# Scanning half as many time steps: odd times by recurrence, even times from them

## The chip, the cores and the metric

The kernel runs on one core of a Trainium2 chip. The metric is the device time of one execution in microseconds. A core has five engines with instruction queues of their own: TensorE (PE in the profile; PEld is its loading of weights), VectorE (DVE), ScalarE (ACT), GpSimd (POOL) and SyncE (SP), and 16 DMA engines that the queues feed. Matmuls write PSUM; the other engines copy results from there to SBUF.

## The reference

Two sequence models over the same input x (2048 times, 1024 channels) are mixed by a gate per time.

```python
def _A_ref(x, Lambda_re, Lambda_im, B_re, B_im, C_re, C_im, log_dt, Dskip):
    Lam, Bmat, Cmat = ...                      # complex
    Lam_bar = jnp.exp(jnp.exp(log_dt) * Lam)
    B_bar = ((Lam_bar - 1.0) / Lam)[:, None] * Bmat
    Bu = jnp.einsum("bld,pd->blp", x + 0j, B_bar)
    for t in range(L):
        h = Lam_bar[None, :] * h + Bu[:, t, :]
        hs.append(h)
    return 2.0 * jnp.einsum("blp,dp->bld", hseq, Cmat).real + x * Dskip[None, None, :]

def _B_ref(q, k, v, shift_k, ssm_k, ssm_D):
    kv = causal_conv4(k, shift_k) * v
    y = long_causal_conv(kv, ssm_k)            # the reference does it by FFT
    return q * (y + kv * ssm_D[None, None, :])

g = _sigmoid((x * gate_w).sum(-1, keepdims=True))
return g * a + (1 - g) * b                     # a = _A_ref(x, ...), b = _B_ref(x, B_k, B_v, ...)
```

The recurrence of `_A_ref` has 1024 complex states. The change concerns how these states are computed.

## The kernel before, in words

The kernel has two halves that overlap for some 40 us. `put` chains every instruction to the one before it on its engine, so each engine works in the order of the program.

**The convolution half** (to about 200 us) computes `_B_ref` by transforms that are matmuls, for eight blocks of 128 channels. `products` multiplies spectra on DVE, `inverse` transforms back (`psz` to `cv`), and the result goes to a scratch in DRAM (`cv_scr`). In the same loop `turn_table` (line 393) builds, for each of the eight groups of 128 states (`pi`), the tables `TC`, `TS` (cosine and sine of the turned angle at each of the 512 times of a block) and `TCi`, `TSi`, the same tables times the factor of the inputs (`c2r`, `c2i`). The latter need two products `m` and an accumulating DMA (`gather`) from POOL.

**The scan half** works on four time blocks `tb` of 512 times and four groups `g` of 256 states, so there are 16 scans.

- `Bu(tb, g)` (652): 32 matmuls of 512 columns on TensorE, 16 for each half `j` into one PSUM tile, and two copies by ACT into `U`. PSUM has four tiles of this size (`ps2`).
- `scan(tb, g, fin)` (663): DVE turns `U` by `TCi`, `TSi` (`A`), which makes the recurrence real; then four `tensor_tensor_scan` instructions of 512 columns (`W`); then it turns back by `TC`, `TS` into the states `hb`. `carry` brings the last state of a block into the next. `scan` is a generator: its steps interleave two scans on DVE. No instruction of ACT is in it.
- `Cy(tb, tl)` (755): 32 matmuls with the states of all four groups as weights, for 128 times, and a copy by ACT times the gate (`scale_a`).
- `scale_b` (ACT) and `finish` (DVE, POOL's DMA, output) mix in the other half; `gate` makes the gate; `load_xT` and `load_CT` are transposing DMAs on SP.

The order is written out by hand at the end: Bu(0,3), Bu(1,0), two gates, Bu(1,1) to Bu(1,3), then a loop over k of 12 passes, with scan k+4, Cy(k), `scale_b(k+1)` and Bu two blocks ahead. Bu ends in pass 7. The last time block's Cy is spread over its groups.

```python
    def advance(j):
        step(scans[j])
        if j + 1 < NS:
            step(scans[j + 1])
        run(scans[j])
    ...
        advance(k + NG)
        Cy(tb, st)
        if k + 1 < NS - NG:
            scale_b(k + 1)
        if tb + 2 < NTB:
            Bu(tb + 2, st)
```

Small tiles come from pools with a few buffers: `wu` (4, for `U` and others), `wk` (3, for the scan's intermediates), `hb` (8).

Of the kernel before, what the change touches and what calls it, by code (L numbers as in the profile page):

```python
# [20 lines left out]
def kernel(  # L21
# [43 lines left out]
    PAD = 16  # L65

# [10 lines left out]
    wu = pool("wu", 4)  # L77
# [60 lines left out]
    m_pool = h3pool(h3, "m", 1)  # L138
# [73 lines left out]
    def load_xT(tb, home=None, halves=(0, 1)):  # L212
        if 0 in halves:
            xTs[tb] = (home or xt_pool).tile([128, ND, TB], BF16, name="xT", tag="xT")
        for h in halves:
            t0 = tb * TB + h * 256
            load_t(xTs[tb][:, :, h * 256:(h + 1) * 256], xf[t0:t0 + 256, :])
# [119 lines left out]
    rv, thn, c2r, c2i, mc2i = small("rv"), small("thn"), small("c2r"), small("c2i"), small("mc2i")  # L337
    TCS = rot_pool.tile([128, NP, 2, TB], BF16, name="TCS")
    TCSi = rot_pool.tile([128, NP, 2, TB], BF16, name="TCSi")
    TC, TS = TCS[:, :, 0], TCS[:, :, 1]  # L340
    TCi, TSi = TCSi[:, :, 0], TCSi[:, :, 1]
# [7 lines left out]
    def state_params():  # L349

        dtv = small("dtv")
        act(dtv, logdt, func=ACT.Exp)
        abv = pair("abv")
        tt(abv, bc(dtv[:, None], [128, 2, NP]), pcol[:, 1:3], ALU.mult)
        act(rv, abv[:, 0], func=ACT.Exp)
        ts(thn, abv[:, 1], 1.0 / TWO_PI, None, ALU.mult)
# [23 lines left out]
        tt(e[:, 0], rv, co[:, 0], ALU.mult)  # L380
        tt(e[:, 1], rv, si[:, 0], ALU.mult)
        ts(e[:, 2], e[:, 0], -1.0, None, ALU.add)
        ts(e[:, 0], e[:, 0], -1.0, None, ALU.add)
# [6 lines left out]
        for o, i, f in ((c2i, p2, 2.0), (mc2i, p2, -2.0), (c2r, p1_, 2.0)):  # L390
            put("dve", V.scalar_tensor_tensor, out=o, in0=i[:, 0], scalar=f, in1=invden, op0=ALU.mult, op1=ALU.mult)

    def turn_table(pi, home):


        hr = home([128, 2, TB], F32, "hr")
        h, rq = hr[:, 0], hr[:, 1]
        act(h, trow[0], func=ACT.Identity, scale=thn[:, pi:pi + 1])
        act(rq, trow[0], func=ACT.Identity, scale=thn[:, pi:pi + 1], bias=magic)
# [5 lines left out]
        act(TS[:, pi], rq, func=ACT.Sin, scale=-TWO_PI)  # L405
        act(TC[:, pi], h, func=ACT.Sin, bias=pih, scale=-TWO_PI)
        yield
# [3 lines left out]
        yield  # L411
        act(flat(TCSi[:, pi]), flat(TCS[:, pi]), func=ACT.Identity, scale=c2r[:, pi:pi + 1])
        gather(flat(TCSi[:, pi]), flat(m))
# [4 lines left out]
    eos, kss = {}, {}  # L418

# [205 lines left out]
    hbs = {}  # L625
    WL, init = {}, {}
# [14 lines left out]
    def carry(tb):  # L641
        q1 = consts.tile([128, 2, NP], F32, name="q1", tag="q1")
        q2 = consts.tile([128, 2, NP], F32, name="q2", tag="q2")
        w = WL[tb - 1]
        tt(q1, w, bc(cs["cU"][:, None, :], [128, 2, NP]), ALU.mult)
        tt(q2, w, bc(cs["sU"][:, None, :], [128, 2, NP]), ALU.mult)
        tt(init[tb][:, 0], q1[:, 0], q2[:, 1], ALU.add)
        tt(init[tb][:, 1], q1[:, 1], q2[:, 0], ALU.subtract)

    Us = {}  # L650
# [12 lines left out]
    def scan(tb, g, fin):  # L663


        last = tb == NTB - 1 and g == NG - 1
        U = Us.pop((tb, g))
        A = w4([128, 2, 2, TB], BF16, "A")
        W = None

        for js in ([slice(0, 1), slice(1, 2)] if last else [slice(0, 2)]):
            g2 = slice(2 * g + js.start, 2 * g + js.stop)
            full = [128, 2, js.stop - js.start, TB]
            Aj, Uj = A[:, :, js], U[:, :, js]
            tt(Aj, bc(TCi[:, g2][:, None], full), Uj, ALU.mult)
            if js.start == 0:
                yield
            b = w4([128, 2, 2, TB], BF16, "trn")[:, :, js]
            tt(b, bc(TSi[:, g2][:, None], full), Uj, ALU.mult)
            if js.start == 0:  # L680
                if g == 0 and tb > 0:
                    carry(tb)
                step(fin)
            tt(Aj[:, 0], Aj[:, 0], b[:, 1], ALU.add)
            tt(Aj[:, 1], b[:, 0], Aj[:, 1], ALU.subtract)
            if W is None:
                W = w4([128, 2, 2, TB], BF16, "W")
            for j in range(js.start, js.stop):
                pi = 2 * g + j
                for c in range(2):  # L690
                    put("dve", V.tensor_tensor_scan, out=W[:, c, j], data0=bc(rv[:, pi:pi + 1], [128, TB]),
                        data1=A[:, c, j], initial=0.0 if tb == 0 else init[tb][:, c, pi:pi + 1],
                        op0=ALU.mult, op1=ALU.add)
            if js.start == 0:
                run(fin)
                hbs[tb, g] = s5p["hb"][(tb * NG + g) % 8 > 2].tile([128, 2, 2, TB], BF16, name="hb")
            hb = hbs[tb, g][:, :, js]
            Wj = W[:, :, js]
            tt(hb, bc(TC[:, g2][:, None], full), Wj, ALU.mult)
            if tb < NTB - 1:  # L700
                copy(WL[tb][:, :, g2], Wj[:, :, :, TB - 1])
            b = w4([128, 2, 2, TB], BF16, "trn")[:, :, js]
            tt(b, bc(TS[:, g2][:, None], full), Wj, ALU.mult)
            if not last:
                yield
            tt(hb[:, 0], hb[:, 0], b[:, 1], ALU.add)
            tt(hb[:, 1], hb[:, 1], b[:, 0], ALU.subtract)
# [6 lines left out]

    def loads(t_):
        rows = slice(t_ * 128, (t_ + 1) * 128)
# [20 lines left out]
    def Cy_g(tb, tl, ps, g, last, by_half=False):  # L737
        tsl = slice(tl * 128, (tl + 1) * 128)
# [22 lines left out]
    def finish(t_, ps=None):  # L761

        rows = slice(t_ * 128, (t_ + 1) * 128)
# [39 lines left out]
    copy(trow[0], iota_i32([128, TB], [[1, TB]], 0, 0, "row"))  # L803
# [115 lines left out]
    with tc.tile_pool(name="fin", bufs=1, side="right") as fin:  # L919
# [30 lines left out]
    def load_CT(pi):  # L950
        for c, src in enumerate((A_C_re, A_C_im)):
            load_t(CT[pi][:, c], src[:, pi * 128:(pi + 1) * 128])

    s5p = {}
    wk = pool("wk", 3)

    s5p["hb"] = pool("hb3", 3), pool("hb5", 5)
# [7 lines left out]
    for pi in range(NP):  # L965
        load_CT(pi)
    move(drow, bc(A_Dskip.rearrange("(o d) -> o d", o=1), [128, D]))
    loads(0)
    Bu(0, 3)
    Bu(1, 0)  # L970
    gate(0)
    gate(1)
    for g in range(1, NG):
        Bu(1, g)
    scale_b(0)

    NS = NTB * NG
    scans = [scan(j // NG, j % NG, finish(j - NG - 1) if j > NG else none) for j in range(NS)]

    def advance(j):  # L980
        step(scans[j])
        if j + 1 < NS:
            step(scans[j + 1])
        run(scans[j])

    step(scans[0])
    for j in range(NG):
        advance(j)
# [21 lines left out]
    pss = []  # L1010
    for tl in range(4):
        ps = ps2([128, 2, 512], "psy")
        halves = [(slice(h * 512, h * 512 + 512), ps[:, h]) for h in range(2)]
        pss.append(([ps[:, 0], ps[:, 1]], halves if tl == 3 else [(slice(0, D), flat(ps))]))
    for g in range(NG - 1):
        for tl in range(4):
            Cy_g(tb, tl, pss[tl][0], g, False)
    run(finish(t0 - 1))
    fins = []
    for tl in range(4):  # L1020
        fins.append(finish(t0 + tl, None if tl == 1 else pss[tl][1]))
        step(fins[tl])
    for tl in range(4):
        Cy_g(tb, tl, pss[tl][0], NG - 1, True, tl == 3)
        if tl == 1:
# [30 lines left out]
```

## Time and profile before

| | before |
|---|---|
| runs shown, median | 414.21 us |
| runs shown, lowest and highest | 414.06, 427.37 us |
| profiled execution, span from first to last instruction | 413.4 us |
| TensorE busy | 404.2 us, 2377 matmuls |
| VectorE busy | 398.3 us, 470 instructions |
| ScalarE busy | 254.9 us, 307 instructions |
| GpSimd busy | 52.4 us |
| mean granted TensorE clock | 0.999 |

The page gives the profiled execution's span and no other time of it; the median of the runs is 0.8 us above that span. Busy time counts the union of an engine's instructions. A profile line of a group reads: engine, operation, output and input by the program's names, shapes, count, then busy us, mean ns of one, and the idle time of the engine just before them with what ended it. A line of the timeline has its start and length first. `psy` are the matmuls of Cy, `bu` those of Bu, `psz` those of `inverse`. As one helper records all instructions of an engine, the line number says little and the tile names are read.

### The profile page before, as it was taken

What the parts mean: (1) busy time and instruction counts of PE and PEld (TensorE: products, weight loads), DVE (VectorE), ACT (ScalarE), POOL (GpSimd) and SP (SyncE); (2) the same over time, 40 slices, a digit from 0 to 9 for tenths busy, and PEclk for the clock granted to TensorE, in tenths of its full rate; (3) what the DMA queues carried; (4) which work ended last, traced back from release to release, by engine and by line L of the source; (5) the groups of instructions that cost most, each with busy time, mean ns of one, the idle gap of its engine ahead of it and who ended that gap; (6) DMA issues with size and microseconds to landing.
All of it is one profiled execution on the core that took longest, in us unless ns stands there. A gap on an engine that the chain in (4) does not pass through costs nothing.

```text
span 413.4 us, 6089 instructions
## 1 busy us (share of the span) xinstructions
PE 404.2 (98%) x2377; PEld 202.2 (49%) x2377; DVE 398.3 (96%) x470; ACT 254.9 (62%) x307; POOL 52.4 (13%) x74
## 2 busy tenths in 40 slices
PE   7999999999999999999999999999999999999995
PEld 4556454554646464444445444444444444444442
DVE  7899999999999999999999999999999999999964
ACT  4898979999999999889223235432542344387001
POOL 3010020202020202001000000101100110133100
PEclk9999999999999999999999999999999999999999
DMA  7768099998999994795199981533955564498422
GB/s 154 154 142 204 10 177 227 215 136 168 217 194 235 190 144 101 155 192 133 33 190 188 175 187 27 124 77 81 203 122 133 117 139 127 78 203 175 106 51 102
DMA packets 126302, 59.79 MB, mean 145 GB/s; under 512 B 106041, under 2 KB 112705, under 8 KB 126274
## 3 DMA queue, kind: packets, MB, share of 16 engines
q1 hardware_dynamic: 117664, 42.22, 47.2%
q0 software_dynamic: 8528, 17.17, 25.1%
q8 instruction: 18, 0.29, 0.3%
q14 instruction: 10, 0.08, 0.1%
q10 hardware_dynamic: 82, 0.02, 0.0%
HBM read 12.86 MB, written 8.39 MB: 51 GB/s over the span
## 4 chain that ended last, share of the span: by engine, by line
PE 64%; DVE 27%; issue 4%; ACT 2%; DMA 1%; ACTq 0%; DVEq 0%
PE psy L91 27%; PE bu L91 27%; DVE wkh L91 8%; DVE BT L91 7%; DVE G L91 6%; PE psz L91 5%; DVE t L91 3%; PE psk L91 2%; DVE ks L91 2%; PE taps L91 1%; DVE ev L91 1%; PE psv L91 1%; PE p L91 1%; DMA rows<-in_A_Lambda_im_dram 1%; PE foldk L91 1%
## 5 line engine op out<-in xcount | busy, mean ns | idle before, releaser
L91 PE MATMUL bu<-xT,BT 128*128 128x512 bf16 x512 | 112.5, 379 | 0.0
L91 PE MATMUL psy<-CT,hb 128*128 128x512 bf16 x512 | 112.0, 379 | 0.0
L91 PEld LDWEIGHTS <-BT 128*128 128x128 bf16 x512 | 50.0, 98 | 60.2
L91 PEld LDWEIGHTS <-hb 128*128 128x128 bf16 x512 | 49.9, 98 | 60.0
L91 ACT ACTIVATE U<-bu 128x1024 bf16<-128x1024 f32 x32 | 32.4, 1020 | 48.2 <-PE bu L91 45.8
L91 DVE TENSOR_TENSOR_SCAN W<-rv,init,A 128x512 bf16<-128x512 f32 x48 | 57.7, 1262 | 0.0
L91 PE MATMUL psz<-G,SI 128*128 128x512 bf16 x128 | 48.5, 379 | 1.9 <-DVE G L91 1.9
L91 PE MATMUL psz<-G,CI 128*128 128x512 bf16 x128 | 48.5, 379 | 0.0
L91 ACT ACTIVATE ga<-psy,gcols 128x1024 bf16<-128x1024 f32 x8 | 8.9, 1113 | 46.3 <-PE psy L91 46.3
L91 PE MATMUL taps<-dg,kT 128*128 128x128 bf16 x512 | 31.8, 226 | 0.0
L91 PEld LDWEIGHTS <-kT 128*128 128x128 bf16 x512 | 30.6, 101 | 0.7
L91 ACT ACTIVATE Vh<-psv 128x1024 bf16<-128x1024 f32 x32 | 30.3, 1041 | 0.0
L91 POOL DMA_DIRECT2D pbb<-gd x12 | 10.3, 856 | 131.5 <-ACT gd L91 119.4
L91 PE MATMUL psk<-eok,CF 128*128 128x512 bf16 (+1 forms) x96 | 25.7, 361 | 0.4 <-ACT eok L91 0.4
L91 PE MATMUL psk<-eok,SF 128*128 128x512 bf16 (+1 forms) x96 | 24.2, 361 | 0.0
L91 ACT ACTIVATE BT<-psy,gcols 128x1024 bf16<-128x1024 f32 x5 | 5.6, 1113 | 29.9 <-PE psy L91 29.9
L91 PEld LDWEIGHTS <-SF 128*128 128x128 bf16 x160 | 15.7, 98 | 16.0 <-issue 0.6
L91 PEld LDWEIGHTS <-CF 128*128 128x128 bf16 x160 | 15.3, 98 | 14.4
L91 DVE TENSOR_TENSOR wkh<-BT,Vh 128x3072 bf16<-128x3072 bf16 (+4 forms) x20 | 21.8, 1112 | 0.0
L91 DVE TENSOR_TENSOR wkh<-Kh,Vh 128x3072 bf16<-128x3072 bf16 (+2 forms) x16 | 21.3, 1352 | 0.0
L91 PEld LDWEIGHTS <-CI 128*128 128x128 bf16 x128 | 12.5, 98 | 17.9 <-issue 3.3
L91 DVE TENSOR_TENSOR hb<-TCS,W 128x2048 bf16<-128x2048 bf16 (+1 forms) x17 | 19.8, 1162 | 1.2
(148 smaller groups left out, 654.9 us busy)
## 6 DMA issues: line engine op xcount, KB each, us to landing
G<-wkh POOLq DMA_DIRECT2D x6, 768.0 KB, 7.2
cv_scr<-cv SPq DMA_DIRECT2D x16, 256.0 KB, 6.3
v<-in_B_v_dram SPq DMA_DIRECT2D x3, 1024.0 KB
pbb<-cv_scr SPq DMA_DIRECT2D x12, 256.0 KB, 3.2
xr<-in_A_x_dram SPq DMA_DIRECT2D x12, 256.0 KB, 3.6
pbb<-gd POOLq DMA_DIRECT2D x12, 256.0 KB, 3.9
TCSi<-m POOLq DMA_DIRECT2D x8, 256.0 KB, 7.5
ga<-xr POOLq DMA_DIRECT2D x8, 256.0 KB, 3.3
```

The costliest lines, as they stand in the source:

```text
L91: i = f(*a, **kw)
```

## The change

The recurrence now runs over the odd times of a block only (256 instead of 512), with the squared factor (`r2`): the input of an odd step is the odd U plus lambda times the even U before it. The even states come afterwards: the even U plus lambda times the odd state before. Both products with lambda (`by_lam`: R from U, ahead of the scan; Q from the odd states, behind it) are four ACT instructions of 512 columns each. The even states of scan i are finished (`evens`) on DVE inside scan i+1. The factor of the inputs, formerly in `TCi`, `TSi`, is multiplied into C once (`turn_C`: four `tensor_scalar` of 1024 columns on DVE and an accumulating DMA of 512 KB per state group). The times of a block are stored with even and odd times apart, so x is loaded, and the output stored, with every second row. C is loaded before the last `inverse`.

The diff, cut to its core:

```diff
-    wu = pool("wu", 4)
+    wu = pool("wu", 6)
 ...
-            load_t(xTs[tb][:, :, h * 256:(h + 1) * 256], xf[t0:t0 + 256, :])
+            load_t(xTs[tb][:, :, h * TH:(h + 1) * TH], xf[tb * TB + h:(tb + 1) * TB:2, :])
 ...
     def turn_table(pi, home):
-        m = m_pool.tile([128, 2, TB], BF16, name="m")
-        act(m[:, 0], TS[:, pi], func=ACT.Identity, scale=c2i[:, pi:pi + 1])
-        act(m[:, 1], TC[:, pi], func=ACT.Identity, scale=mc2i[:, pi:pi + 1])
-        act(flat(TCSi[:, pi]), flat(TCS[:, pi]), func=ACT.Identity, scale=c2r[:, pi:pi + 1])
-        gather(flat(TCSi[:, pi]), flat(m))
 ...
+    def turn_C(pi):
+        n = w4([128, 2, D], BF16, "n")
+        k = slice(pi, pi + 1)
+        for c in range(2):
+            ts(n[:, c], CT[pi][:, 1 - c], mc2i[:, k], None, ALU.mult)
+        for c, f in enumerate((c2r, mc2r)):
+            ts(CT[pi][:, c], CT[pi][:, c], f[:, k], None, ALU.mult)
+        gather(CT[pi].rearrange("p c d -> p (c d)"), n.rearrange("p c d -> p (c d)"))
 ...
+    def by_lam(o, src, g):
+        for q in range(2):
+            for j in range(2):
+                act(o[:, q, :, j], src[:, :, j], func=ACT.Identity, scale=cs["lam"][:, q, 2 * g + j:2 * g + j + 1])
+    def ahead(i, home=None):
+        tb, g = divmod(i, NG)
+        Rs[i] = (home or r4)([128, 2, 2, 2, TH], BF16, "R")
+        by_lam(Rs[i], Us[tb, g][:, :, :, 0:TH], g)
+    def plus(o, a):
+        tt(o[:, 0], o[:, 0], a[:, 1, 1], ALU.subtract)
+        tt(o[:, 1], o[:, 1], a[:, 1, 0], ALU.add)
+    def turned(t, g):
+        p = w4([128, 2, 2, 2, TH], BF16, "P")
+        tt(p, TCS of the group, t, ALU.mult)          # one product of 2048 columns
+        return p
+    def evens(i):
+        ...
+        hb, q = hbs[tb, g], Qs.pop(i)
+        he = hb[:, :, :, HP + TH:]
+        tt(he, Us.pop((tb, g))[:, :, :, 0:TH], q[:, 0], ALU.add)
+        yield
+        plus(he, q)
+    def scan(i, fin):
+        U, R = Us[tb, g], Rs.pop(i)
+        v = R[:, 0]
+        tt(v, U[:, :, :, TH:], v, ALU.add)
+        if g == 0 and tb > 0:
+            carry(tb)
+        step(fin)
+        plus(v, R)
+        back = evens(i - 1)
+        p = turned(v, g)
+        step(back)
+        A, W = p[:, 0], p[:, 1]
+        tt(A[:, 0], A[:, 0], W[:, 1], ALU.add)
+        tt(A[:, 1], A[:, 1], W[:, 0], ALU.subtract)
+        run(back)
+        ...                                            # four tensor_tensor_scan of 256 columns
+        run(fin)
+        ...                                            # last odd state of the block before, by ACT
+        p = turned(W, g)
+        if tb < NTB - 1:
+            copy(WL[tb][:, :, 2 * g:2 * g + 2], W[:, :, :, TH - 1])
+        tt(ho[:, 0], p[:, 0, 0], p[:, 1, 1], ALU.subtract)
+        tt(ho[:, 1], p[:, 0, 1], p[:, 1, 0], ALU.add)
+        Qs[i] = w4([128, 2, 2, 2, TH], BF16, "Q")
+        by_lam(Qs[i], hb[:, :, :, HP - 1:HP + TH - 1], g)
 ...
         Bu(0, 2)
-        run(inverse(c))
-    h3.close()
+        ahead(0, u4)
 ...
+    for pi in range(NP):
+        load_CT(pi)
+    run(inverse(c))
+    h3.close()
-    wk = pool("wk", 3)
+    wk = pool("wk", 5)
+    wr = pool("wr", 2)
 ...
+    def advance(i):
+        if i + 1 < NS:
+            ahead(i + 1)
+        scan(i, finish(i - NG - 1) if i > NG else none)
+    advance(0)
     Bu(0, 3)
+    advance(1)
+    for pi in range(4):
+        turn_C(pi)
     Bu(1, 0)
     gate(0)
     gate(1)
-    for g in range(1, NG):
-        Bu(1, g)
+    advance(2)
+    for pi in range(4, NP):
+        turn_C(pi)
+    Bu(1, 1)
+    advance(3)
+    Bu(1, 2)
+    Bu(1, 3)
     scale_b(0)
 ...
+    run(evens(NS - 1))
+    order = 2, 3, 0, 1                                 # last block: odd times first
```

More of the change, by code (lines that the diff above doesn't have):

```diff
@@ L335, in small @@
         return consts.tile([128, NP], F32, name=name)
[L337 to L341, printed above, removed]
+    rv, r2, thn = small("rv"), small("r2"), small("thn")
+    c2r, mc2r, mc2i = small("c2r"), small("mc2r"), small("mc2i")
+    TCS = rot_pool.tile([128, 2, NP, TH], BF16, name="TCS")
     drow = rot_pool.tile([128, D], BF16, name="drow")
@@ L355, in state_params @@
         act(rv, abv[:, 0], func=ACT.Exp)
+        act(r2, abv[:, 0], func=ACT.Exp, scale=2.0)
         ts(thn, abv[:, 1], 1.0 / TWO_PI, None, ALU.mult)
@@ L379, in state_params @@
         e = pair("e", 3)
[L380 to L383, printed above, removed]
+        lam = cs["lam"] = pair("lam")
+        tt(lam[:, 0], rv, co[:, 0], ALU.mult)
+        tt(lam[:, 1], rv, si[:, 0], ALU.mult)
+        copy(e[:, 1], lam[:, 1])
+        ts(e[:, 2], lam[:, 0], -1.0, None, ALU.add)
+        ts(e[:, 0], lam[:, 0], -1.0, None, ALU.add)
         p2 = pair("p2")
@@ L389, in state_params @@
         tt(p1_[:, 0], p1_[:, 0], p1_[:, 1], ALU.add)
-        for o, i, f in ((c2i, p2, 2.0), (mc2i, p2, -2.0), (c2r, p1_, 2.0)):
+        for o, i, f in ((mc2i, p2, -2.0), (c2r, p1_, 2.0), (mc2r, p1_, -2.0)):
             put("dve", V.scalar_tensor_tensor, out=o, in0=i[:, 0], scalar=f, in1=invden, op0=ALU.mult, op1=ALU.mult)
     def turn_table(pi, home):
-        hr = home([128, 2, TB], F32, "hr")
+        hr = home([128, 2, TH], F32, "hr")
         h, rq = hr[:, 0], hr[:, 1]
-        act(h, trow[0], func=ACT.Identity, scale=thn[:, pi:pi + 1])
-        act(rq, trow[0], func=ACT.Identity, scale=thn[:, pi:pi + 1], bias=magic)
+        odd = trow[0][:, TH:]
+        act(h, odd, func=ACT.Identity, scale=thn[:, pi:pi + 1])
+        act(rq, odd, func=ACT.Identity, scale=thn[:, pi:pi + 1], bias=magic)
         yield
@@ L661, in Bu @@
         Us[tb, g] = U
[L663 to L688, printed above, removed]
-                pi = 2 * g + j
[L690 to L707, printed above, removed]
@@ new lines, in turned @@
+    def turned(t, g):
+        full = [128, 2, 2, 2 * TH]
+        p = w4([128, 2, 2, 2, TH], BF16, "P")
+        tt(p.rearrange("p s c j t -> p s c (j t)"),
+           bc(TCS[:, :, 2 * g:2 * g + 2].rearrange("p s j t -> p s (j t)")[:, :, None], full),
+           bc(t.rearrange("p c j t -> p c (j t)")[:, None], full), ALU.mult)
+        return p
+    def evens(i):
+        if i < 0:
+            yield
+            return
+        tb, g = divmod(i, NG)
+        hb, q = hbs[tb, g], Qs.pop(i)
+        he = hb[:, :, :, HP + TH:]
+        tt(he, Us.pop((tb, g))[:, :, :, 0:TH], q[:, 0], ALU.add)
+        yield
+        plus(he, q)
@@ new lines, in scan @@
+    def scan(i, fin):
+        tb, g = divmod(i, NG)
+        U, R = Us[tb, g], Rs.pop(i)
[12 more added lines that the diff above has]
+        run(back)
+        for c in range(2):
+            for j in range(2):
+                pi = 2 * g + j
+                put("dve", V.tensor_tensor_scan, out=W[:, c, j], data0=bc(r2[:, pi:pi + 1], [128, TH]),
+                    data1=A[:, c, j], initial=0.0 if tb == 0 else init[tb][:, c, pi:pi + 1],
+                    op0=ALU.mult, op1=ALU.add)
+        run(fin)
+        hb = hbs[tb, g] = s5p["hb"][i % 8 > 1].tile([128, 2, 2, HP + TB], BF16, name="hb")
+        ho = hb[:, :, :, HP:HP + TH]
+        last = hb[:, :, :, HP - 1:HP]
+        if tb == 0:
+            put("pool", nc.gpsimd.memset, last, 0.0)
+        else:
+            act(last, hbs[tb - 1, g][:, :, :, HP + TH - 1:HP + TH], func=ACT.Copy)
+        p = turned(W, g)
[5 more added lines that the diff above has]
+        by_lam(Qs[i], hb[:, :, :, HP - 1:HP + TH - 1], g)
@@ L761, in finish @@
     def finish(t_, ps=None):
-        rows = slice(t_ * 128, (t_ + 1) * 128)
+        rows = rows_of(t_)
         pbb, xr = ios.pop(t_)
@@ L802 @@
     trow[0] = consts.tile([128, TB], mybir.dt.float16, name="row")
-    copy(trow[0], iota_i32([128, TB], [[1, TB]], 0, 0, "row"))
+    copy(trow[0], iota_i32([128, 2, 2, 128], [[1, 2], [TH, 2], [2, 128]], 0, 0, "row").rearrange("p a b t -> p (a b t)"))
     sp = state_params()
@@ L964 @@
     load_xT(2, xt2_pool)
-    for pi in range(NP):
-        load_CT(pi)
     move(drow, bc(A_Dskip.rearrange("(o d) -> o d", o=1), [128, D]))
     loads(0)
+    NS = NTB * NG
+    def advance(i):
[3 more added lines that the diff above has]
+    advance(0)
     Bu(0, 3)
+    advance(1)
+    for pi in range(4):
+        turn_C(pi)
     Bu(1, 0)
@@ L972 @@
     gate(1)
-    for g in range(1, NG):
-        Bu(1, g)
-    scale_b(0)
[L977 to L988, printed above, removed]
+    advance(2)
[5 more added lines that the diff above has]
+    Bu(1, 3)
+    scale_b(0)
     for k in range(NS - NG):
```

54 lines of the change are left out of this document (29 added, 25 removed).

## The prediction

> **What bounds the kernel now.** I read the busy time by engine first, then TensorE's own waits, then the timeline of each engine from 165 to 262 us (where the convolution half hands over to the scan half) and from 340 us on, then the groups kept apart by shape, for prices.
>
> ```profile
> PE 404.2 (98%) x2377; PEld 202.2 (49%) x2377; DVE 398.3 (96%) x470; ACT 254.9 (62%) x307; POOL 52.4 (13%) x74
> ```
> ```profile
> PE psz L91 <- DVE G L91: 1.9, 5, 0.7
> PE p L91 <- DMA rows<-in_A_Lambda_im_dram: 1.5, 1, 1.5
> ...
> PE psk L91 <- ACT eok L91: 0.4, 1, 0.4
> ```
> TensorE (PE) is the bound: 404.2 of 413.4 us, and a block of 32 matmuls takes 6.91 us in the chain of waits, 0.216 us each, wherever it stands. About 4 us of its idle time lie ahead of its work and 4.2 us behind its end at 409.2 us; between them lie the waits above, all before 155 us. From there to 409.2 us it never stops. The change touches no matmul's size or number, so VectorE (DVE) time that is saved can bring back 2 us at most, while every new TensorE wait after 155 us is added in full. So I looked for waits.
>
> ```profile
> 241.29 1.23 DVE L91 TENSOR_TENSOR hb<-TCS,W 128x2048 bf16<-128x2048 bf16 x1
> ...
> 244.78 1.28 DVE L91 TENSOR_TENSOR hb<-hb,trn 128x1024 bf16<-128x1024 bf16 x2
> ```
> ```profile
> 241.67 7.07 PE L91 MATMUL psy<-CT,hb 128*128 128x512 bf16 x32
> ```
> These are the last states of time block 0, hb(0,3), and the first Cy, which reads group 3 in its last quarter, from 246.9 us. The states are done at 246.1: the hand-over has 0.8 us of room. A DVE chain that ends later there stops TensorE.
>
> ```profile
> 191.34 0.72 ACT L91 ACTIVATE m<-TCS,c2i 128x512 bf16<-128x512 bf16 x1 [1.00 <-DMA TCSi<-m]
> ...
> 193.62 2.82 ACT L91 ACTIVATE U<-bu 128x1024 bf16<-128x1024 f32 x3
> 198.83 1.02 ACT L91 ACTIVATE U<-bu 128x1024 bf16<-128x1024 f32 x1 [2.38 <-PE bu L91]
> ```
> ScalarE (ACT) works in program order: the first half of Bu(0,1) was done at 188.3 us, and its copy ran at 193.6, behind a table's waiting product. Until now nothing in ACT's scan-half queue waits for DVE, so that such a hold costs nothing. There are four PSUM tiles, one for each half of a Bu and one for each Cy; a held copy stops TensorE when all four are full.
>
> **Prices.** A DVE instruction starts 0.08 us before the last one's end (0.11 later if it needs that one's result).
>
> ```profile
> L91 DVE TENSOR_TENSOR_SCAN W<-rv,A 128x512 bf16<-128x512 f32 x16 | 18.2, 1202 | 0.0
> ...
> L91 DVE TENSOR_SCALAR dg<-ident,pcol 128x128 bf16<-128x128 bf16 x12 | 2.2, 278 | 0.1
> ...
> L91 DVE TENSOR_TENSOR hb<-hb,trn 128x512 bf16<-128x512 bf16 x4 | 1.5, 420 | 0.1
> ...
> L91 DVE TENSOR_SCALAR NSF<-SF 128x512 bf16<-128x512 bf16 x1 | 0.3, 284 | 0.0
> ```
> ```profile
> L91 ACT ACTIVATE m<-TCS,c2i 128x512 bf16<-128x512 bf16 x8 | 5.9, 736 | 1.0 <-DMA TCSi<-m 1.0
> ```
> Shapes that the trace shows: products of 2048 columns 1.14 us apart, of 1024 0.61, of 512 0.35; a 512-column ACTIVATE with a column as scale 0.61. Not shown, so bounded: (a) a recurrence over 256: from 0.35 (the spacing of a 512-column product) to 1.14 (a whole 512 step, if all of it were fixed). Products of 512 and 1024 columns leave 0.155 us fixed; taking that from 1.202 and halving the rest gives 0.68 long, 0.60 apart; taken, nearest to half the 512 row. (b) a 1024-column multiply by a column (turn_C): from 0.16 (the four dg in 0.65 us) to 0.61 (the 1024 product). From tiny multiplies of 0.17 us to NSF's 0.284 the columns cost 0.23 ns each; 896 more than dg make 0.16 into 0.37 to 0.40; I take 0.40.
> The Trainium skill, "VectorE: DVE Perf Modes", section on the perf-mode tier table, gives such a one-source bf16 multiply of 2048 columns 693 ns, twice the rate of a product; I estimate from it 0.42 us for 1024, 0.31 apart. By it turn_C costs 10 us instead of 12.8 and the time below is 2 us lower; NSF's 284 ns against 420 for the product of the same 512 columns agrees in kind, and I keep the rows.
>
> **The change, part by part.** *Convolution half.* The turn tables shrink to 256 columns and lose m, TCSi and the TCSi gather: eight times 0.27 us of DVE (0.60 to 0.33) and about 3.3 us of ACT per table. One pass lasts 21.57 us on DVE (49.71 to 71.28 in the chain) and 21.3 on TensorE, so DVE's 0.27 in six passes takes away most of the psz waits: -1.5 us (0 to -2). ACT's part is worth nothing; it ran beside.
> *Loads.* xT with every second row is not shown at all: between nothing and twice the 7.7 us to landing; xT(0) lands 20 us and xT(1) 40 us ahead of use, so nothing either way. The 16 CT transposes now go out before inverse(7)'s two cv moves, and behind them on SP wait xT(2), drow and loads(0). They wait for products(7)'s room, 195.5 us, and at 23 us for the 16 end at 219; cv lands 6.3 us later, before hb(2), which takes its room, is written at 234, and xT(2) is needed only at 261. Cost: nothing.
> *DVE per group.* Before: 11.75 us (208.35 to 220.09), 12.5 with the output product. After: v 0.61+0.11, plus 0.80, p 1.14, even states 0.61+0.70, A 0.70, four recurrences 2.40, p 1.18, WL 0.08, odd states 0.70: 9.0, and 9.7 later. Saved: some 45 us over 16 groups; turn_C gives back 12.8. None of it is TensorE's.
> *ACT.* 128 more ACTIVATEs, 78 us in idle time, but in a queue with the copies. This is where the time goes.
>
> **Start, on before's clock.** R(0) stands behind the copy of Bu(0,2), 198.8, so it is ready at 202.4; DVE, free at about 197, waits 5.4 us. Odd states of scan 0 end at 210.3. Q(0) on ACT then 212.8, and only then the copies of Bu(0,3), R(2) 217.1. Scan 1 219.3; Q(1) 221.9; copies of Bu(1,0) 222.8 and 223.8. TensorE, done with the gates at 220.9, finds no PSUM tile until then: 2.0 us lost. DVE: turn_C of four, 6.4 us, then scan 2 ends 234.8; Q(2) 237.3, copies of Bu(1,1) 238.3: Bu(1,3) starts 1.6 us late. turn_C of four until 241.2, scan 3 250.2, Q(3) 252.8, copy of Bu(1,2) 253.7. All four tiles hold finished Bu until then: Cy(0,0) starts 8.5 us late. Its group 3 needs the even states of scan 3, made inside scan 4, 255.2; it gets there at 259. Lost: 2.0+1.6+8.5 = 12.2 us (about).
> *Middle.* DVE needs 9.7 us per group, TensorE 13.8; ACT 10 to 12. R(k+5) is behind the U copies of pass k-1, so DVE no longer runs ahead of TensorE; it idles some 4 us per pass. No TensorE wait.
> *Tail.* Let T be the end of Bu(3,3). R(13) follows its copy and two scalings: T+5.6. Then DVE must do scans 13, 14, 15, odd states at T+15.4, T+25.7, T+35.9 (10.3 us apart, as R(14), R(15) come just behind); Q(15) T+38.5. scale_a(11), the copy of the last Cy of block 2, stands behind Q(15): T+39.5. TensorE has four Cy (27.6) and three quarters of the last block, 5.2, in hand, and needs that tile at T+32.7: 6.9 us lost. Before, the same copy had no scan in front of it. After it everything is there; the last 4.2 us stay.
> Sum: 413.4 - 1.5 + 12.2 + 6.9 = 431.0 span. The median of the runs shown, 414.21, is 0.8 over the profiled span: **431.8 us**.
> Bounds: recurrence 0.35 gives 5 us less, 1.14 14 more; multiplies 0.16 3 less, 0.61 6 more; ACTIVATEs 0.50 apart (overlapped) 3 less, 0.72 (not) 4 more.
>
> **Rivals.** *1. A ready copy is not held* (other side). If Bu copies pass waiting Q products, both PSUM waits and the tail go; only the direct chain is left, deciding at 246.9 us: even states of scan 3 at 255.2 stop the first Cy for 8.4. 413.4 - 1.5 + 8.4 + 0.8 = 421.1, not slower by the 2% below. For it: idle ACT time; against: the copy held from 188.3 to 193.6.
> The Trainium skill, "Perfetto Trace Analysis", section on per-engine timelines, calls ACT, DVE and GpSimd strict FIFO, which would exclude this rival; the held copy agrees.
> *2. TensorE is never kept waiting*: the chain from R(0) to the even states takes 44 us instead of 53. With (a) and (b) both at their low ends it would (0.25 x 16 + 0.24 x 32 = 11.7 less) and with the copies free too: 412.7. Against: two extremes at once.
> *3. The gathers into CT are late.* n's five buffers come round: scan 2's p takes the room of the first n, whose gather starts at 221 and must land by 227.4. 768 KB took 7.2 us, 256 KB 3.3 to 7.5; 5.4 taken for 512 KB. At 10 us two groups wait about 4 us each: 440. TensorE's unbroken Bu run at 221 to 241 us speaks for oldest room first, or it would be far worse.
>
> **Chances.** Forecast 0.68, own range 423 to 442 (its bounds, extremes not all at once); rival 1 0.12, rival 2 0.08, rival 3 0.12. The range 419 to 443 takes in rivals 1 and 3 and leaves out rival 2 and the far ends, under 0.2. Two per cent, 8.3 us, is about what a measurement of this kernel can tell from no change. Faster than that, TensorE's 404.2 us nearly forbid: 0.02. Within: rival 2, most of rival 1, the low edge of the forecast: 0.17. Slower: 0.81.
>
> **What will show it.** Right: ACT Q-products waiting for DVE hb; TensorE idle just before Cy(0,0) by some 8 us and again some 7 us in the last block, released by ACT; turn_C multiplies near 0.48 us long, recurrences near 0.68; DVE share near 84%, ACT near 70%. Wrong: unbroken TensorE after 155 us, U copies running ahead of Q products, or waits on CT gathers or xT.

## The result, and the profile after

| | before | after |
|---|---|---|
| runs beside each other, median | 414.21 us | 449.20 us |
| lowest and highest | 413.98, 427.37 us | 440.54, 457.37 us |
| profiled execution: time, span | span 413.4 us | 440.54 us, span 438.8 us |

The change makes the kernel slower: 1.070 times the time before, 95% interval 1.061 to 1.079. (The ratio compares the executions near each kernel's fastest, so it is smaller than the quotient of the medians.) The forecast was 431.8 us, its range 419 to 443. So the forecast failed: it was 17 us below the median, and the median lies 6 us beyond the end of the range. The profiled execution lies inside the range; it is the fastest of the five and 8.7 us faster than the median. All readings below are of it, so they explain its 8.7 us above the forecast and not the median's further 8.7.

The busy times of the page after:

```profile
PE 406.6 (93%) x2339; PEld 201.9 (46%) x2377; DVE 366.7 (84%) x559; ACT 310.0 (71%) x424; POOL 54.1 (12%) x78
```

VectorE did lose work, 398.3 to 366.7 us, and its share and ScalarE's are the forecast ones (84%, 71%). TensorE's busy time rose by 2.4 us with the same matmuls (38 of their records are missing from this trace), and the span by 25.4. TensorE's waits after (releasing engine and tile: us in total, times, longest):

```profile
PE psy L92 <- DVE hb L92: 11.5, 1, 11.5
PE psy L92 <- ACT BT L92: 5.9, 1, 5.9
PE bu L92 <- ACT U L92: 3.8, 2, 2.4
```

Before, none of these existed. Their places are in TensorE's timeline (start, length, what ran, in brackets the idle time before it and what ended it):

```profile
217.15 1.74 PE L92 MATMUL p<-gwb,xT 128*128 128x1 bf16 x64
220.23 0.59 PE L92 MATMUL bu<-xT,BT 128*128 128x512 bf16 x1 [1.35 <-ACT U L92]
...
238.03 7.07 PE L92 MATMUL bu<-xT,BT 128*128 128x512 bf16 x32 [2.42 <-ACT U L92]
256.55 2.29 PE L92 MATMUL psy<-CT,hb 128*128 128x512 bf16 x5 [11.46 <-DVE hb L92]
...
409.50 24.94 PE L92 MATMUL psy<-CT,hb 128*128 128x512 bf16 x102 [5.87 <-ACT BT L92]
```

The reader sees the forecast waits, in their places: ahead of Bu(1,1), ahead of Bu(1,3), a long one ahead of the first Cy, and one in the last block. ScalarE's timeline shows why they are there: at the start Q waits for VectorE, and copies that were long ready (`U`) run right behind it. In the last block Q(15) itself waits only 0.88 us, but the copy `BT` stands behind it.

```profile
234.51 2.56 ACT L92 ACTIVATE Q<-hb,lam 128x512 bf16<-128x512 bf16 x4 [9.30 <-DVE hb L92]
236.97 1.91 ACT L92 ACTIVATE U<-bu 128x1024 bf16<-128x1024 f32 x2
...
253.03 2.57 ACT L92 ACTIVATE Q<-hb,lam 128x512 bf16<-128x512 bf16 x4 [11.69 <-DVE hb L92]
255.50 3.73 ACT L92 ACTIVATE U<-bu 128x1024 bf16<-128x1024 f32 x4
...
405.89 2.56 ACT L92 ACTIVATE Q<-hb,lam 128x512 bf16<-128x512 bf16 x4 [0.88 <-DVE hb L92]
408.36 1.09 ACT L92 ACTIVATE BT<-psy,gcols 128x1024 bf16<-128x1024 f32 x1
```

For the first Cy the view of the waits names `DVE hb` as the releaser, and here it has to be read with care. Near that time VectorE made the even states of scan 3, which this Cy needs only in its last quarter:

```profile
255.84 0.69 DVE L92 TENSOR_TENSOR hb<-U,Q 128x1024 bf16<-128x1024 bf16 x1
...
257.11 0.75 DVE L92 TENSOR_TENSOR hb<-hb,Q 128x512 bf16<-128x512 bf16 x2
```

They were complete at 257.86, 1.3 us after this Cy had begun, so it did not wait for them. What ended at 256.52, just before it began, is the first of the four copies of `U` behind Q(3), which frees a PSUM tile. The same coincidence, to 0.06 us, is in the traces of e2, e5, e6, e8, e9, e10 and e11 below, and in e9 the view itself names the copy (`ACT U`). So VectorE's chain reaches TensorE through the odd states of scan 3, Q(3) and the held copy, as the prediction had it.

Two things in the traces weren't in the forecast's sum. First, VectorE waits for the additions of `n` into CT (the gathers of `turn_C`), three times before the first Cy, 4.4 us in all; the prediction had named such waits as a sign of being wrong (VectorE's timeline):

```profile
226.85 1.23 DVE L92 TENSOR_TENSOR P<-TCS,R 128x2048 bf16<-128x2048 bf16 x1 [1.87 <-DMA CT<-n]
...
235.78 0.88 DVE L92 TENSOR_SCALAR n<-CT,mc2i 128x1024 bf16<-128x1024 bf16 x2 [1.36 <-DMA CT<-n]
...
245.37 1.23 DVE L92 TENSOR_TENSOR P<-TCS,R 128x2048 bf16<-128x2048 bf16 x1 [1.16 <-DMA CT<-n]
```

The DMA issues (count, KB each, median us to landing) give such an addition 9.1 us, where 5.4 was taken:

```profile
CT<-n POOLq DMA_DIRECT2D x8, 512.0 KB, 9.1
```

Second, the granted TensorE clock halves during a long wait and is still half when work resumes. In the windows of 1 us around the first Cy, the columns after the window are its length, busy us (and instructions) of PE, PEld, DVE, ACT and POOL, then the clock, the DMA share and GB/s:

```profile
249.00:250.00 1.00, 0.00 (x0) 0.00 (x0) 1.00 (x3) 0.00 (x0) 0.00 (x0) 1.00 0.98 197
250.00:251.00 1.00, 0.00 (x0) 0.00 (x0) 0.97 (x3) 0.00 (x0) 0.00 (x0) 0.70 1.11 217
251.00:252.00 1.00, 0.00 (x0) 0.00 (x0) 1.00 (x1) 0.00 (x0) 0.00 (x0) 0.50 1.21 242
...
257.00:258.00 1.00, 1.00 (x4) 0.39 (x3) 1.00 (x4) 1.00 (x2) 0.00 (x0) 0.50 0.00 0
...
260.00:261.00 1.00, 1.00 (x5) 0.39 (x4) 0.96 (x2) 1.00 (x2) 0.00 (x0) 0.68 0.00 0
261.00:262.00 1.00, 1.00 (x6) 0.42 (x5) 1.00 (x3) 1.00 (x3) 0.40 (x1) 1.00 0.00 0
```

TensorE stopped at 245.1; the clock fell about 5 us later and came back about 4 us after the restart at 256.55. In between the matmuls run at half their pace: the first Cy ended at 265.5 where 6.91 us per block would have given 263.5.

The 25.4 us of span are therefore, in this execution: the first Cy starts at 256.55 in place of 241.67, +14.9 (the convolution half, which ended 2.0 us earlier, is already in this); half clock in the first Cy, +2.0; the wait in the last block, +5.9; half clock behind it, +2.3 (24.94 us for 102 matmuls, 22.61 at full clock in the second experiment); 0.3 more at the end.

### The profile page after: what moved, and what is told of

It reads as the page before. It is cut to its first block, busy times and chain, and to the rows that moved or that the text cites. A ratio compares the mean times of both kernels' runs of the same rounds, so it can differ in the third digit from the quotient of the medians.

```text
span 438.8 us, 6282 instructions
## 1 busy us (share of the span) xinstructions
PE 406.6 (93%) x2339; PEld 201.9 (46%) x2377; DVE 366.7 (84%) x559; ACT 310.0 (71%) x424; POOL 54.1 (12%) x78
## 4 chain that ended last, share of the span: by engine, by line
PE 42%; DVE 38%; issue 9%; ACT 6%; DMA 4%; ACTq 0%; POOL 0%; DVEq 0%; POOLq 0%
PE psy L92 19%; PE bu L92 17%; DVE wkh L92 8%; DVE BT L92 7%; DVE P L92 7%; DVE G L92 5%; PE psz L92 3%; DVE t L92 2%; DVE hb L92 2%; PE psk L92 2%; DVE ks L92 2%; DMA CT<-n 2%; DVE R L92 1%; ACT R L92 1%; DMA pbb<-gd 1%
## 5 line engine op out<-in xcount | busy, mean ns | idle before, releaser
L92 PE MATMUL psy<-CT,hb 128*128 128x512 bf16 x502 | 115.8, 389 | 18.1 <-DVE hb L92 11.5
L92 ACT ACTIVATE Q<-hb,lam 128x512 bf16<-128x512 bf16 x64 | 41.0, 712 | 25.1 <-DVE hb L92 24.8
L92 ACT ACTIVATE R<-U,lam 128x512 bf16<-128x512 bf16 x64 | 40.8, 716 | 0.0
L92 DVE TENSOR_TENSOR R<-U,R 128x1024 bf16<-128x1024 bf16 x16 | 11.0, 690 | 35.1 <-ACT R L92 35.1
L92 DVE TENSOR_TENSOR_SCAN P<-r,init,P 128x256 bf16<-128x256 f32 x48 | 32.1, 731 | 0.0
L92 PE MATMUL taps<-dg,kT 128*128 128x128 bf16 x512 | 30.0, 219 | 0.0
L92 PEld LDWEIGHTS <-kT 128*128 128x128 bf16 x512 | 28.8, 98 | 0.7
L92 POOL DMA_DIRECT2D pbb<-gd x12 | 10.3, 856 | 129.9 <-ACT gd L92 104.8
L92 ACT ACTIVATE cv<-psz 128x1024 bf16<-128x1024 f32 x16 | 16.4, 1023 | 12.8 <-PE psz L92 12.8
L92 PE MATMUL psk<-eok,CF 128*128 128x512 bf16 (+1 forms) x89 | 24.2, 360 | 0.5 <-ACT eok L92 0.5
L92 DVE TENSOR_TENSOR P<-TCS,R 128x2048 bf16<-128x2048 bf16 x16 | 19.6, 1225 | 3.5 <-DMA CT<-n 3.0
```

Source lines behind the costliest of these rows:

```text
L92: i = f(*a, **kw)
```

## The experiments

The theory, called A below where an expectation names it: at the start VectorE's own chain decides, from R(0) through two times four `turn_C` to the states of scan 3; in the last block ScalarE's order decides, the copy of a finished Cy standing behind Q(15); the late additions and the half clock come on top. The rivals were that held copies decide at the start, that the additions' lateness is only a matter of `n`'s room, and that the clock costs nothing.

**e1_no_turn: `turn_C` left out.**

```diff
-    for pi in range(4):
-        turn_C(pi)
 ...
-    for pi in range(4, NP):
-        turn_C(pi)
```

> Leaves out turn_C altogether (its 32 multiplies and 8 gathers), so the output lacks the factor of the inputs. Theory A (at the start TensorE waits for the VectorE chain up to block 0's states; turn_C and the waits for its gathers are 17 us of that chain): the wait of 11.5 us ahead of the first Cy goes, with it the one of 2.4 ahead of Bu(1,3) and some 2 us at half clock; the tail stays: 440.5 - 16 = about 424.5. Theory B (ScalarE's queue holds the copies of Bu behind Q products, whatever VectorE does): most of the wait stays, 434 or more.

Measured: 424.87 us (424.70 to 425.83), ratio 1.025 (1.023 to 1.027). The wait ahead of the first Cy is gone (Cy starts at 243.20); what is left of TensorE's waits:

```profile
PE psy L92 <- ACT BT L92: 5.8, 1, 5.8
...
PE bu L92 <- ACT U L92: 1.3, 1, 1.3
```

The 424.5 us expected came. So VectorE's chain at the start, with `turn_C` and its additions in it, is worth 15.8 us of span (438.8 - 423.0): 13.35 for the later first Cy, 2.0 for its half clock, the rest in small differences. The tail's wait is independent of it, and stays.

**e2_tail: Q(15) behind the copy of the last Cy of block 2.**

```diff
-        Qs[i] = w4(...)                       # end of scan
-        by_lam(Qs[i], ...)
+    def behind(i): ...                        # the same two lines, called at the end of advance
 ...
         Cy(tb, st)
+        if k == NS - NG - 1:
+            behind(NS - 1)
```

> Same work; in the last pass Q(15) is put behind the copy of Cy(2,3) in ScalarE's queue. Theory A (that copy, held behind Q(15), stops TensorE 5.9 us and the clock then costs 2.4 more): about 432. Rival (the states of the last scan are late anyway and TensorE would stop a little later in the last block): 438 to 441.

Measured: 439.68 us (436.07 to 442.30), ratio 1.059 (1.053 to 1.066). The time is not the 432 expected but in the rival's range, for another reason than the rival's: in the stage itself the gain is plain. From the start of the last run of Cy to the end of the last matmul it takes 58.0 us in place of 63.8, so 5.8 less: 3.5 of wait and 2.3 of half clock.

```profile
413.60 22.61 PE L92 MATMUL psy<-CT,hb 128*128 128x512 bf16 x102 [2.41 <-ACT BT L92]
```

The 2.4 us that remain are ScalarE's own pace: it works without a pause there, 10.3 us for each scan. But in this execution the additions were later still, and took the gain back (VectorE waited 11.4 us for them in three places, 7.0 more than in the first profile):

```profile
234.51 1.23 DVE L92 TENSOR_TENSOR P<-TCS,R 128x2048 bf16<-128x2048 bf16 x1 [9.06 <-DMA CT<-n]
```

The first Cy started at 264.0. The order of ScalarE makes 5.8 us of the tail; the start varies with the additions.

**e3_warm: work for TensorE in the waits.** The second half of Bu(1,3) is computed four times, Cy(2,3) twice; the text on record counts 88 matmuls more, there are 80.

```diff
-            for c in range(2):
+            for c in [0, 1] * (1 + (extra if j == 1 else 0)):      # Bu; extra = 3 in Bu(1,3)
 ...
-        for g in range(NG):
+        for g in [0, 1, 2, 3] * (2 if (tb, tl) == (2, 3) else 1):  # Cy
```

> Same results, more work: Bu(1,3)'s second half is computed four times in place (10.4 us of matmuls in the 11.5 us wait), and Cy(2,3) twice (6.9 us in the wait of 5.9). Theory C (a wait of several us halves TensorE's clock for the first 4 to 5 us of work after it): 2 us less at the start, about 1.5 less in the tail, 437, although 88 matmuls are added; and the runs lie closer together. Rival (the clock is a record only, or falls for another reason): 441 to 442, the tail's 0.9 us of extra matmuls added.

Measured: 448.33 us (443.49 to 455.54), ratio 1.069 (1.067 to 1.072). The first Cy and the tail run at full clock, but VectorE waited 6.0 us for an addition in one place here, so the time tells nothing about the clock. Inconclusive; repeated below without the additions (e10).

**e4_copies_first: at the start each Bu's copies ahead of the Q products.**

```diff
-    advance(0)
+    advance(0, False)                         # scan without its Q
     Bu(0, 3)
-    advance(1)
+    behind(0)
+    advance(1, False)
+    Bu(1, 0)
+    behind(1)
 ...                                           # the same for scans 2 and 3
```

> Same work; in the start each Bu's copies go ahead of the Q products of the scan in front of it. Theory A (VectorE's chain decides): the waits ahead of Bu(1,1) and Bu(1,3) go (3.8 us), but those us are waited ahead of the first Cy instead, and Q(0), Q(1) come up to 3 us later: 438 to 443. Theory B (held copies decide): the wait of 11.5 goes as well, 426 to 430.

Measured: 439.99 us (438.83 to 460.23), ratio 1.061 (1.058 to 1.063). The waits ahead of Bu(1,1) and Bu(1,3) are gone, and come back in the first Cy:

```profile
248.21 2.29 PE L92 MATMUL psy<-CT,hb 128*128 128x512 bf16 x5 [7.82 <-ACT U L92]
...
256.23 1.90 PE L92 MATMUL psy<-CT,hb 128*128 128x512 bf16 x8 [2.77 <-DVE hb L92]
265.56 3.39 PE L92 MATMUL psy<-CT,hb 128*128 128x512 bf16 x8 [7.43 <-DVE hb L92]
```

TensorE is ahead by more and waits by more, and here VectorE's chain does decide: the last wait ends with the even states of scan 3. The time came in the range of theory A. But this does not show that held copies cost nothing at the start of the changed kernel, for e4 also lengthened the chain: VectorE waited 9.0 us for additions in place of 4.4, and 2.5 us for Q(0), which now stands behind copies. Less these 7.1 us, e4's first Cy would have ended at 261.7 in place of 268.8 (an estimate), against 265.5 after the change. So of the start's delay some 4 us may belong to the copy held in front of the first Cy; no run separates them.

**e5_no_gather: the additions into CT left out.**

```diff
-        gather(CT[pi].rearrange("p c d -> p (c d)"), n.rearrange("p c d -> p (c d)"))
```

> Leaves out only the 8 gathers that add n into C (the 32 multiplies stay), so the output lacks that part of the factor. Theory D (VectorE waits 4.4 us in the profiled run and up to 11.4 in others for the gathers that still hold n's buffers; these waits also make the runs differ by 17 us): no such wait, the first Cy where the prediction had it, near 252; span 438.8 - 4.4 = 434 to 435, time about 436, and runs within 1% of each other. What is left above the forecast of 431.8 is then the clock, about 4. Rival (the runs differ through the clock alone): same spread as the changed kernel, 440 to 457.

Measured: 437.44 us (437.33 to 438.56, 0.3% apart), ratio 1.052 (1.047 to 1.057). VectorE's waits for DMA at the start vanish: from R(0) to the even states of scan 3 its chain is shorter by 4.5 us, the 4.4 that it had waited. (In this execution R(0) itself was 1.2 us later, so that the first Cy starts only 3.3 us earlier, at 253.27, and the time is 1.4 us over the 436 expected.) And SyncE's queue shows that the additions had slowed something else, too, the load of xT(2): its two instructions took 14.91 us to issue after the change, here 6.56.

**e6_R0, e7_lam_dve, e8_n_hb: three ways around single waits**, run beside e5.

```diff
+        ahead(0, u4)                          # e6: R(0) ahead of Bu(0,2)
         Bu(0, 2)
-        ahead(0, u4)
 ...
-                act(o[:, q, :, j], ..., scale=cs["lam"][...])            # e7: by_lam on VectorE
+                ts(o[:, q, :, j], ..., cs["lam"][...], None, ALU.mult)
 ...
-        n = w4([128, 2, D], BF16, "n")                                   # e8: n in one of six hb tiles
+        n = s5p["hb"][1].tile([128, 2, D], BF16, name="hb")
```

> Same work; R(0) goes ahead of Bu(0,2) in ScalarE's queue, so scan 0 may start when VectorE is free (194.8 instead of 198.9). Theory A (the VectorE chain decides the start): 4 us less at the first Cy when the gathers take equally long; since these differ from run to run, read from the profile: the first Cy's start less VectorE's waits for CT gathers, 252.2 in the changed kernel, falls to 248. Rival (the gathers wait for the load of C, which does not move, or copies are held elsewhere): no change there.

Measured: 441.62 us (440.00 to 441.83). The wait ahead of Bu(1,1) is gone, the first Cy starts at 257.03, with 5.4 us of waits for additions in VectorE's chain. Less these that is 251.6, not the 248 expected: the expectation failed. R(0)'s wait of 4.0 us is gone, but VectorE waits 1.3 us for TensorE's `psz` ahead of the odd states of scan 0, and 2.0 us for R(1), which stands behind a copy of `cv`. As in e4, a wait removed ahead of the first Cy comes back there.

> Same results; the products with lambda (R and Q) move from ScalarE to VectorE as 128 multiplies of 512 columns, by an estimate from the 0.40 spacing of 1024 columns 0.28 each, some 35 us. Theory A2 (in the tail ScalarE's queue, with R, Q and scale_b at 10.3 us a pass, holds the last copy): TensorE's tail wait of 5.9 goes, its waits ahead of Bu(1,1) and Bu(1,3) go; the start's chain loses R(0)'s wait of 4 and gains 4 x 2.2 and waits for the first Cy some 5 us later; sum 433 to 438 with gathers as in the profiled run. Rival (VectorE's 11 to 12 us per group become the bound): tail wait stays or grows, 442 or more.

Measured: 439.85 us (439.53 to 440.39). The tail's wait is gone (the last 251 matmuls in the trace, 55.4 us, run without a stop), which shows that ScalarE's queue made it. At the start VectorE's chain grew; TensorE's waits for hb rose from 11.5 to 19.8 us. One loss was traded for the other, and the time is 2 us above the range expected.

> Same work and results; n lies in buffers of hb that are still unused at the start (io is placed ahead of them), so the scan's products P do not wait for a gather. Theory D: as without gathers, about 436, runs within 1%. Rival (slow gathers then hold Cy itself, which reads C): the wait moves to the first Cy, 440 or more and spread as before.

Measured: 443.20 us (437.95 to 458.67). VectorE's products wait for no addition now, but the additions land still later (median 20.9 us, and xT(2)'s load takes 31.67 us to issue beside them), and the waits have moved on: 2.6 us of TensorE's Cy and 2.5 us of VectorE for CT, and ScalarE waits 8.9 us for `pbb`, whose load stands behind xT(2) on SP. The expectation of 436 us failed: `n`'s room alone isn't the cause; the transfers themselves are late.

**e9_late_xT2: the load of xT(2) after the last `turn_C`.**

```diff
+            if after is not None:             # in load_xT: the load waits for this copy
+                for h in halves:
+                    copy(xTs[tb][:, 0, h * TH:h * TH + 1], after)
 ...
-    load_xT(2, xt2_pool)
 ...
     for pi in range(4, NP):
         turn_C(pi)
+    load_xT(2, xt2_pool, after=mc2i[:, 0:1])
```

> The strided transposing load of xT(2) is issued behind the scaling of the last four matrices of C (about 243 us) in place of 218; the computation is whole. Theory A (the additions into CT are late because they share the 16 DMA engines with that load, whose two instructions took 14.9 us to issue): the additions land in about 5 us, VectorE no longer waits for them (4.4 us in the first profile of the change), the time is about 437 and the runs lie within 1 %. Rival (the additions are slow by themselves, or by the loads of CT): landing 8 us and more, waits of 4 us and up, 440 to 449 with runs several per cent apart. Rival (xT(2) itself comes too late for Bu(2,0)): TensorE waits for xT near 262 us, and the time rises by that wait.

Measured: 439.53 us (437.98 to 441.29), ratio 1.059 (1.055 to 1.063). The first four additions now hold up no product (a multiply into `n` still waits 2.1 us). The last four run beside the moved load instead, which took even longer to issue (SyncE's queue):

```profile
243.93 16.81 SPq L92 DMA_TRANSPOSE xT<-in_A_x_dram  x2
```

and a product of scan 4, at 260 us, waited 5.3 us for one of them. The runs lie within 0.8%, as theory A expected; the time, 2.5 us over the 437 it gave, does not decide, since the contention was moved and not removed (median to landing 8.6 us, where about 5 was expected).

**e10_no_gather_busy: e5, with TensorE kept busy in its two long waits.** The edit is e3's with `extra = 2`, on top of e5's.

> The additions into CT are left out, as in the kernel without them (437.4), and TensorE is given work in place of its two long waits: the second half of Bu(1,3) is computed three times (32 matmuls more, about 7.1 us in a wait of 8.9) and Cy(2,3) twice (32 more, 7.1 us in a wait of 6.4). Theory A (beside the waits, the half clock costs 2.0 us at the first Cy and 2.4 in the tail): clock 1.00 in both places, 437.4 - 2.0 - 2.4 + 0.6 = about 433.6. Rival (the half clock costs nothing that another engine wouldn't set): 437 to 438.

Measured: 433.63 us (432.93 to 434.45), ratio 1.045 (1.042 to 1.048). Sixty-four matmuls more, and 3.8 us less than e5, as expected. The windows of 5 us from 250 on, first e5, then e10:

```profile
250.00:255.00 5.00, 1.73 (x5) 0.63 (x5) 4.93 (x14) 5.00 (x8) 0.00 (x0) 0.50 0.00 0
255.00:260.00 5.00, 4.78 (x15) 1.89 (x15) 4.87 (x9) 5.00 (x8) 0.90 (x1) 0.62 0.05 9
```
```profile
250.00:255.00 5.00, 3.06 (x15) 1.26 (x13) 4.97 (x11) 5.00 (x7) 0.00 (x0) 1.00 0.00 0
255.00:260.00 5.00, 4.95 (x24) 2.29 (x24) 4.23 (x8) 4.97 (x9) 0.90 (x1) 1.00 0.21 35
```

From the first Cy to the next block of Bu e5 takes 9.60 us (253.27 to 262.87) and e10 6.91 (252.63 to 259.54): 2.7 us of half clock, where 2.0 were expected. The last matmul ends 5.4 us earlier in e10's profile (427.1 against 432.5), of which 0.6 is an earlier start, 2.7 the first Cy, and 2.1 the tail. The half clock is a cost of its own, behind both waits. (The profiled execution of e5 is the slowest of its four, so the profiles differ by 5.4 us and the medians by 3.8.)

**e11_xT2_behind_tail: e2's order, and xT(2)'s load behind the last addition** (as in e9, but the small copy is GpSimd's and reads CT, so that the load waits for the addition).

> Two edits in one kernel, the computation whole: xT(2)'s load waits, through a small copy on GpSimd, for the last addition into CT (issued near 250 us, 7.5 us to landing, needed near 262), and in the tail the Q products of scan 15 stand behind the copy of the last Cy of block 2. Theory A (additions and xT(2) slow each other on the DMA engines; the tail is an order of ScalarE; both add up): VectorE waits for additions 2 us or less instead of 4.4 before the first Cy, so 440.5 - 2.4 - 5.8 = about 432, runs within 1 %. Rival (the additions are slow by themselves): waits of 4 us and more stay, 435 to 440 with the spread. Rival (xT(2) then comes too late): TensorE waits for xT near 262 us, and 432 rises by that wait.

Measured: 435.31 us (433.51 to 437.09, 0.8% apart), ratio 1.046 (1.042 to 1.051). Both rows move the way that theory A expected, though not all the way:

```profile
227.46 1.23 DVE L92 TENSOR_TENSOR P<-TCS,R 128x2048 bf16<-128x2048 bf16 x1 [0.52 <-DMA CT<-n]
...
237.10 0.88 DVE L92 TENSOR_SCALAR n<-CT,mc2i 128x1024 bf16<-128x1024 bf16 x2 [2.07 <-DMA CT<-n]
```
```profile
252.42 6.04 SPq L92 DMA_TRANSPOSE xT<-in_A_x_dram  x2
```

VectorE waits 2.6 us in place of 4.4, where 2 or less were expected; the load issues in 6.0, and TensorE never waits for xT. So the load of xT(2) accounts for about 1.8 of the 4.4 us, if these two executions are alike in the rest. The time is 3 us over the expected 432, and the trace shows where: the convolution half ended 2.0 us later than in the first execution after the change, about when it ended before the change. That takes back the 1.8 us, so that the profile's gain, 438.8 to 433.1, is the tail's 5.8 alone. The half ended at other times in other executions too (the gates start between 217.2 and 219.4 us, latest in the two kernels with xT(2) moved); why was not tried.

This is the fastest version with the whole computation, and 4.6% slower than before. A version that beats the kernel before wasn't found: with every start and tail wait gone, TensorE's 404 us and the 8 us around them are still 412, which before has already.

## Why the prediction was wrong, and what of it held

*The mechanism held.* The bound, the four places of TensorE's waits and ScalarE's held copies, in front of the first Cy too, came as written; so did the prices (recurrence over 256: 0.61 apart against 0.60; `turn_C`'s multiply 0.48 long, 0.40 apart, as taken; ScalarE's product 0.61 apart). Rival 1, that a ready copy is not held, is excluded by the held copies of the timeline, and e7 removes the tail by emptying ScalarE's queue. Rival 2 fails with them. The prediction's estimate from the perf-mode tier table of the Trainium skill's "VectorE: DVE Perf Modes" was 0.42 us for the multiply; the trace measures 0.48, so the rows were right to be kept.

*The start's chain was right to the wait for the additions.* The odd states of scan 3 were forecast at 248.7 us (250.2 on before's clock, 1.5 earlier) and came at 252.9, or 248.5 without the 4.4 us of waits for additions; the first Cy, behind Q(3) and a copy, was forecast at 252.2 and came at 256.55. (The three losses at the start add up to 12.1; the prediction's 12.2 is rounded.)

*Step that failed: the term of the additions, taken as 5.4 us to landing and so as no wait.* It measured 9.1 us in the first profile, single ones up to 18.9 in e2, and VectorE waited 4.4 to 11.4 us for it (e2: 9.06 + 1.16 + 1.18). This was rival 3, at 0.12 and 440 us: it was the actual course. That its 440 us met the profiled 440.5 is luck: it priced the waits at two of about 4 us, they came to 4.4 in all, and the half clock, which it did not have, made up the rest. The 5.4 was taken between rows of 256 KB (3.3 to 7.5 us) and 768 KB (7.2), as if each addition stood alone. They come four in a row, 1.5 to 2.0 us apart, and even in the quietest stretch (the second four of e11) landed after 4.8, 6.0, 6.7 and 7.8 us. In the first profile, where 16 transposes of C, the strided xT(2) and the additions fall within 60 us with all DMA engines busy (share 1.0 to 1.2 in the windows), they took 7.4 to 12.0. The prediction's working set xT(2)'s new place against its use at 261 us, where it indeed cost nothing, and never against the additions that it runs beside.

*Term left out: the half clock.* Every TensorE wait was added at its bare length. The rule was to be had: the Trainium skill, "TensorE: Matmul & The Clock Gate", Part 1, lets the clock fall to half after an idle window of about 3.4 us and asks for about as long at work to restore it. The trace agrees in kind, with 5.3 and 3.8 us to the fall and 4.1 and 4.7 us to the recovery. So about 4 us at half pace lose 2: two waits forecast as 8.5 and 6.9 us should have been charged some 2 us each; 4.3 were measured, and e10 shows the cost by removing it.

*The tail* was forecast at 6.9 and measured 5.9; *the convolution half* -1.5 forecast, -2.0 measured here and about nothing in e11. Together, in span: 431.0 forecast, + 4.4 (first Cy later) + 4.3 (half clock) - 1.0 (tail) = 438.7, measured 438.8.

*What stays open.* No execution near the median was profiled, so what the median has beyond the profiled execution, 8.7 us, has no trace. That it comes from the additions too is suggested, not shown. The kernels without additions (e1, e5, e10), the two with xT(2) moved and e7, whose additions began behind xT(2)'s load, lie within 0.2 to 0.8%, while five of the kernels with both side by side spread over 1.4 to 4.9%. And e2's profile, with 7.0 us more of such waits, is 7.5 us longer than the first profile less the tail's 5.8. Against it: e6, with both side by side, lies within 0.4%, and single runs of the kernel before, which has no additions into CT, reach 427 us as well.

## What to carry to other kernels

A change that takes work off an engine that isn't the bound is worth only what its new waits don't cost: here 32 us less VectorE work bought nothing, and one ScalarE product in the middle of a copy queue cost 5.8 us of TensorE in the tail. In a kernel like this one, charge a long TensorE wait with about 2 us on top for the half clock: waits of 3.4 us (e6) and more cost 1.6 to 2.7 us here, wherever the cost can be read by itself, waits of 1.9 to 2.4 us ahead of Bu or Cy nothing. Price a set of transfers together, at the load of the stretch in which they run, and not one of them at its time alone. When a load is moved past others, look for what it now runs beside, not only whether it is in time.

## What the runs showed of the hardware

- Accumulating moves slow a transposing load beside them. The two instructions of xT(2) took 5.69 to 6.78 us to issue without additions (e1, e5, e10) and 6.04 and 6.46 behind or ahead of them (e11, e7), but 14.89 to 31.67 beside them (after and e2, e3, e6, e8, e9); only in e4, where just its second half met them, 7.47.
- Additions of 512 KB, four in a row, landed 2.6 to 2.9 us apart in the quietest stretch (e11), though issued 1.5 to 2.0 us apart: 4.8 us for the first, 7.8 for the last. Beside other transfers they were later, up to 23.9 us (e8). The load of xT(2) is not the only one that delays them: in e11, without it, the first four took 6.5 to 11.3 us, and in e4, where it was over at 226.5 and plain loads of `xr` and `pbb` ran, 12.3 to 17.7.
- A TensorE that waited for long lost half its clock, in the first profile 5.3 us after the last matmul ahead of the first Cy and 3.8 us after it in the tail; it came back 4.1 and 4.7 us after the restart (from the mean clock in windows of 1 us). The one-column matmuls of the gates count for little, it seems: with a wait of only 1.3 us behind them the mean clock from 220 to 225 us was 0.66 to 0.69 in seven profiles (after, e1, e2, e3, e5, e8, e10), 0.83 in e11 and 1.00 in e9; with none (e4, e6, e7) it was 1.00. The same wait thus costs or doesn't. The Trainium skill, "TensorE: Matmul & The Clock Gate", Part 1, calls the window in which activity is judged a free-running one; these rows would fit that and do not show it.
